# Second MoE's combined weights in rings of their own, loads two steps ahead of the sums, and an eight-column rope scratch

## The chip, the cores and the metric

The kernel runs on one core of one Trainium2 chip. The metric is the device time of one launch in microseconds (us), the median of several runs. The engines are named as in the profile: PE (matrix), PEld (its weight loads), DVE (vector), ACT (scalar), POOL (GpSimd) and SP, which issues nearly all transfers (DMAs). Each engine takes its instructions strictly in the order of its own queue: one that waits holds back everything behind it on that engine.

## The reference

Attention with rotary embedding (4 batches, 8 heads, 576 positions, head size 64), then two feed-forward blocks (MoE here) over 2304 tokens of width 512.

```python
q_rot, k_rot = (rotate(q), rotate(k))                      # rope
attn = softmax(q_rot @ k_rot.T / sqrt(64));  x = attn @ v  # 4 x 8 heads
x = reshape(x, (2304, 512))
h = maximum(maximum(x @ w1, x @ w2), x @ w3)               # first MoE, 768 wide
y = h @ w_out
h = y @ w_in2;  g = h / (1 + exp(-h))                      # second MoE, 2048 wide
out = g @ w_out2
```

Weights arrive as 64-bit floats.

## The kernel before

**Matmuls in halves.** All large products run in fp16 with a high and a low part for each operand, three passes for each product. The second MoE uses seven block products in place of eight (a scheme of Strassen's kind), so its weights are needed as eight 128-column blocks for each piece: four as stored and four sums or differences of these (`SUMS`).

**Attention phase.** `attention()` is a generator over 80 tiles of 128 queries. In each step PE computes the scores of a tile (L424, L427), DVE takes the row maximum (`nb`, L437), ACT the exponentials (`e`, L444), one step later ACT scales them (L456), and from batch 1 on four DMAs and a DVE transpose (`pt`, L495 and L517) turn them for the product with v (`xp`, L558, L562). Between these PE runs groups of the first MoE (`moe1`, L657), whose results are taken out of PSUM by ACT and DVE (`t`, L674 and L676; `h`, L682 and L683; `y`, L700). The PSUM ring of these groups has two banks, so a group waits until the one before the last is taken out.

**Weights prepared beside it.** In the same steps the second MoE's weights are narrowed from 64 bits: `narrow_w2` loads a piece (`z64`), ACT takes its upper half (L228), POOL (L230) and DVE (L239, L240) add lower bits, ACT measures it (`junk`, L154), and it goes to a DRAM scratch, `zwi` for the first weight matrix, `zwo` for the second. When the scale of the first is known, from tile 53 of 80 on, `prep_w8(1.7)` makes the combined weights: 16 items, a new one every 1.7 steps. An item loads four blocks from `zwi` (two DMAs, L950), POOL makes four sums (L926), ACT casts four blocks to the high part (`cast_high`, L930, placed behind the latest exponential), DVE makes the low part (`cast_low`, L934), a DMA stores both in `w8scr` (L961), and the same is done with the four sums. Before the change the eight blocks of an item are one tile `z8` in a ring of two, the first cast goes to `w8o`, which has one buffer, and the second cast goes over the first half of the same `z8` (rows of the profile call `z8` and `z64` both `z`). The offsets of an item's steps are 0 (load), 1 (sums), 1.1 and 2 (first high and low), 2.1 and 3 (second high and low).

**After attention** the last batch's first MoE and then the second MoE (`moe2`, L1053, L1085, L1148) run with PE nearly without a gap; eight loads from `w8scr` (`w8_load`) are issued at the end of attention, and later ones in step with their use.

**Order.** The program is written in the order of these generators; a scheduler then sets each engine's queue, so a transfer or a sum whose inputs are there can stand far ahead of its place in the text. `tc.issue_after(x)` keeps an instruction behind x. A `Ring` hands out its buffers in turn, and a write to a buffer waits for all readers of what was in it.

**Rope.** `qk_rope` loads nothing itself; it rotates q and k of a pair of heads in three parts of 8, 8 and 2 columns of 64 (`rope_steps`: three instructions a part, L353, L354, L357), for batch 0 partly on DVE, else on POOL. Its scratch `w` is one tile of 18 columns.

Of the kernel before, what the change touches and what calls it, by code (L numbers as in the profile page):

```python
# [17 lines left out]
P = 128  # L18
# [4 lines left out]
def fused_kernel(  # L23
# [48 lines left out]
    small = Ring(ctx, "small", 4)  # L72
    junk_p = Ring(ctx, "junk", 1)
# [19 lines left out]
    z8_p, w8o_p = right("z8_p", 2), right("w8o", 1)  # L93
# [88 lines left out]
    class Weights:  # L182
# [68 lines left out]
        def row_max(self, lo=0, n=None, ma=None):  # L251
            ma = ma or self.maxima(lo, n or self.m)
            m1 = small.tile([P, 1], F32, tag="wm1", name="wm1")
            nc.vector.tensor_reduce(out=m1, in_=ma, op=ALU.max, axis=AX.X)
            return m1
# [66 lines left out]
    def v_scale(b):  # L322
        ma = vmax_t.pop(b)
        m = small.tile([P, 1], F32, tag="vm1", name="vm1")
        nc.vector.tensor_reduce(out=m, in_=ma, op=ALU.max, axis=AX.X)
        vmax_t[b] = all_max_a(m)
# [5 lines left out]
    def qk_rope(b, hp):  # L332
        t = raw_t[b, hp]
        w = w_p.tile([P, 18, D], F32, tag="w", name="w")
        if b:
            with tc.issue_after(last["pool"]):
                return rope_steps(t, w, nc.gpsimd, ((0, 8), (8, 16), (16, 18)))
        if hp == 1:
            with tc.issue_after(last["kd"]):
                rope_steps(t, w, nc.vector, ((8, 16), (16, 18)))  # L340
            return rope_steps(t, w, nc.gpsimd, ((0, 4), (4, 8)))
        if hp == 0:
            return rope_steps(t, w, nc.vector, ((8, 16), (0, 8), (16, 18)))
        return rope_steps(t, w, nc.gpsimd, ((0, 8), (8, 16), (16, 18)))

    def rope_steps(t, w, eng, parts):

        tt, at_ = eng.tensor_tensor, lambda c: 4 if c == 16 else c // 2 % 4
        for lo, hi in parts:
            r, v = t[:, lo:hi, :], w[:, lo:hi, :]  # L350
            t4, w4 = (x.rearrange("p (a h) d -> p a h d", h=2) for x in (r, v))
            sin2, cos2 = (x[:, at_(lo):at_(lo) + (hi - lo) // 2, :].unsqueeze(2).to_broadcast([P, (hi - lo) // 2, 2, D]) for x in (sin_sb, cos_sb))
            tt(out=w4, in0=t4, in1=sin2, op=ALU.mult)  # L353
            tt(out=t4, in0=t4, in1=cos2, op=ALU.mult)  # L354
            u4 = r.rearrange("p a (t e) -> p a t e", t=2)
            w4 = v.rearrange("p a (t e) -> p a t e", t=2)
            x = tt(out=u4, in0=u4, in1=w4[:, :, ::-1, :], op=ALU.add)  # L357
        return x
# [577 lines left out]
    def prep_w8(step):  # L936
# [4 lines left out]
        def item(k):  # L941
# [3 lines left out]
            def load():  # L945
                z[0] = z8_p.tile([P, 8, P], F32, tag="z8", name="z8")
                for i in range(2):
                    o = (f + i * HB) * DM
                    x = zscr["wi"][:, o:o + DM].rearrange("p (a c n) -> p a c n", a=2, c=2)[:, :, c]
                    nc.sync.dma_start(out=z[0][:, i:i + 3:2], in_=x)  # L950

            def high(a):
                if a == 0:
                    w[a] = w8o_p.tile([P, 2, 4, P], F16, tag="w8o", name="w8o")
                else:
                    w[a] = flat(z[0][:, 0:4]).bitcast(F16).rearrange("p (x a n) -> p x a n", x=2, n=P)
                cast_high(flat(w[a][:, 0]), flat(z[0][:, a:a + 4]), sw, exps[-1])

            def low(a):
                cast_low(flat(w[a][:, 1]), flat(w[a][:, 0]), flat(z[0][:, a:a + 4]), sw, last["max"])  # L960
# [3 lines left out]
            for d, fn in ((0, load), (1, lambda: combine(z[0], SUMS)), (1.1, lambda: high(0)), (2, lambda: low(0)), (2.1, lambda: high(4)), (3, lambda: low(4))):  # L964
# [279 lines left out]
    wraw = ExitStack()  # L1244
    wraw_p = Ring(wraw, "wraw", 2)

    def pre_down():

        if x_p.get(1) is None:
# [4 lines left out]
            mpools.append(Ring(left, "y_p", 2))  # L1254

# [85 lines left out]
    b_now[0] = 0  # L1341
    attn_pools.close()
# [84 lines left out]
```

## Time and profile before

| | |
|---|---|
| median of 3 runs | 991.97 us (989.47 to 992.7) |
| profiled execution, its own time | 989.2 us |
| its span, first to last instruction | 987.4 us |
| mean granted TensorE clock | 0.974 of full speed |
| busy in the span: PE / DVE / ACT / POOL | 907.6 / 700.4 / 604.0 / 492.2 us |
| attention phase with combined weights being made | about 380 to 569 us |
| first matmul of the second MoE | 644.2 us |

The profile is of one execution; its own time stands 1.8 us above its span, and 2.8 us below the median of the runs. Busy shares are means over stages with different limits, so the argument below goes by stretches and by single waits.

### The profile page before, as it was taken

What the parts mean: (1) busy time and instruction counts of PE and PEld (TensorE: products, weight loads), DVE (VectorE), ACT (ScalarE), POOL (GpSimd) and SP (SyncE); (2) the same over time, 40 slices, a digit from 0 to 9 for tenths busy, and PEclk for the clock granted to TensorE, in tenths of its full rate; (3) what the DMA queues carried; (4) which work ended last, traced back from release to release, by engine and by line L of the source; (5) the groups of instructions that cost most, each with busy time, mean ns of one, the idle gap of its engine ahead of it and who ended that gap; (6) DMA issues with size and microseconds to landing.
All of it is one profiled execution on the core that took longest, in us unless ns stands there. A gap on an engine that the chain in (4) does not pass through costs nothing. (4 is left out here: it accounts for less than half of the span.)

```text
span 987.4 us, 19157 instructions
## 1 busy us (share of the span) xinstructions
PE 907.6 (92%) x6802; PEld 669.8 (68%) x6802; DVE 700.4 (71%) x1231; ACT 604.0 (61%) x1381; POOL 492.2 (50%) x546
## 2 busy tenths in 40 slices
PE   4776998899997999889979899999998999999997
PEld 2343664566664666556645577788887888888886
DVE  5779888777787677868677548764777857856554
ACT  2888577757776677768867625464564544544442
POOL 5835494972546403423233207463678368365264
PEclk9598999999999999999999899999999999999999
DMA  6943035859999775979989673174444344334101
GB/s 155 293 126 106 22 102 132 180 118 198 185 198 188 192 119 134 226 207 216 227 197 198 177 218 113 60 230 133 151 158 133 97 155 134 97 112 135 60 1 43
DMA packets 185198, 146.29 MB, mean 148 GB/s; under 512 B 51216, under 2 KB 168720, under 8 KB 185104
## 3 DMA queue, kind: packets, MB, share of 16 engines
q1 hardware_dynamic: 183600, 144.36, 57.5%
q8 instruction: 54, 0.88, 0.4%
q10 hardware_dynamic: 1504, 0.72, 0.3%
q14 instruction: 40, 0.33, 0.1%
HBM read 90.51 MB, written 26.21 MB: 118 GB/s over the span
## 5 line engine op out<-in xcount | busy, mean ns | idle before, releaser
L657 PEld LDWEIGHTS <-w 128*128 128x128 f16 x1632 | 161.1, 99 | 70.8 <-issue 26.8
L657 PE MATMUL m<-x,w 128*128 128x256 f16 (+1 forms) x1356 | 190.8, 291 | 18.5 <-ACT t L674 10.0
L1148 PEld LDWEIGHTS <-g 128*128 128x128 f16 x1485 | 145.3, 98 | 16.8
L1085 PEld LDWEIGHTS <-w8s 128*128 128x128 f16 x1344 | 131.1, 98 | 16.1 <-issue 0.9
L444 ACT ACTIVATE e<-s,nb 128x576 f32<-128x576 f32 x144 | 105.1, 735 | 34.4 <-DVE nb L437 31.7
L437 DVE TENSOR_REDUCE nb<-s 128x2 f32<-128x1152 f32 (+1 forms) x80 | 98.5, 1232 | 35.2 <-PE s L427 27.1
L926 POOL TENSOR_TENSOR z<-z 128x128 f32<-128x128 f32 (+1 forms) x96 | 62.4, 668 | 121.9 <-DMA z<-zwi 71.9
L456 ACT ACTIVATE e<-e,rec 128x576 f32<-128x576 f32 x144 | 104.1, 767 | 13.9 <-DVE rec L454 13.5
L230 POOL TENSOR_SCALAR z<-z 128x256 uint16<-128x256 uint16 x64 | 51.9, 810 | 107.8 <-ACT z L228 80.6
L562 PE MATMUL xp<-pt,vd 128*64 128x256 f32 (+1 forms) x512 | 79.4, 416 | 0.9 <-DVE pt L517 0.9
L427 PE MATMUL s<-T 64*128 64x512 f32 x256 | 78.6, 684 | 0.0
L517 DVE STREAM_TRANSPOSE pt<-pt 128x1024 f32<-128x1024 f32 (+1 forms) x60 | 67.7, 1128 | 9.7 <-DMA pt<-e 9.7
L1099 POOL TENSOR_TENSOR z<-t 128x256 f32<-128x256 f32 x32 | 27.1, 846 | 87.3 <-DVE t L1091 52.2
L353 POOL TENSOR_TENSOR w<-qk,sin_sb 128x512 f32<-128x512 f32 (+2 forms) x44 | 44.8, 1036 | 41.8 <-DMA qk<-in_q_dram 13.4
L1037 DVE SCALAR_TENSOR_TENSOR g<-gsum,sg,g 128x1024 f16<-128x1024 f32 x36 | 49.1, 1371 | 22.0 <-ACT g L1036 21.6
L657 PE MATMUL m<-h,wo 128*128 128x256 f16 (+1 forms) x448 | 63.9, 292 | 0.4 <-DVE wo L177 0.2
L1036 ACT ACTIVATE g<-gsum,sg 128x1024 f16<-128x1024 f32 x36 | 40.8, 1140 | 36.5 <-POOL gsum L1032 36.5
L657 PEld LDWEIGHTS <-wo 128*128 128x128 f16 x512 | 50.5, 100 | 17.6 <-issue 1.9
L562 PEld LDWEIGHTS xp<-pt,vd 128*64 128x64 f32 x512 | 35.5, 137 | 36.8 <-issue 14.7
L240 DVE SCALAR_TENSOR_TENSOR z<-z,z 128x256 int32<-128x256 int32 x64 | 36.8, 575 | 19.2 <-POOL z L230 18.2
L1148 PE MATMUL b<-w,g 128*128 128x256 f16 x376 | 48.5, 273 | 0.0
L1148 PE MATMUL a<-w,g 128*128 128x256 f16 x376 | 47.9, 273 | 0.0
(254 smaller groups left out, 1956.5 us busy)
## 6 DMA issues: line engine op xcount, KB each, us to landing
w8s<-w8scr SPq DMA_DIRECT2D x64, 448.0 KB, 4.4
pt<-e SPq DMA_DIRECT2D x192, 128.0 KB, 3.9
z<-in_moe_w_in_dram SPq DMA_DIRECT2D x32, 256.0 KB, 3.8
z<-in_moe_w_out_dram SPq DMA_DIRECT2D x32, 256.0 KB, 3.9
w<-in_moe_w_dram SPq DMA_DIRECT2D x6, 768.0 KB, 5.5
wo<-in_moe_w_dram SPq DMA_DIRECT2D x6, 768.0 KB, 4.8
qk<-in_q_dram SPq DMA_DIRECT2D x32, 128.0 KB, 3.4
vd<-in_v_dram SPq DMA_DIRECT2D x16, 256.0 KB, 3.2
```

Source lines behind the costliest of these rows:

```text
L230: nc.gpsimd.tensor_scalar(out=q[:, :, 2], in0=q[:, :, 1], scalar1=step, scalar2=off, op0=ALU.mult, op1=ALU.add)
L427: last["s"] = last["score"] = nc.tensor.matmul(s[:, o:o + 512], qs[r], kt[r], start=True, stop=True).ins
L437: x = nc.vector.tensor_reduce(out=nb[:, 0:m], in_=both(s, 0, 960, 576) if m > 1 else s[:, 0:576], op=ALU.max, axis=AX.X, negate=True)
L444: x = nc.scalar.activation(out=e[:, HK[g]], in_=s[:, SK[g]], func=AF.Exp, bias=nb[:, g:g + 1], accum_out=sm[:, g:g + 1])
L456: nc.scalar.activation(out=e[:, HK[g]], in_=e[:, HK[g]], func=AF.Copy, scale=r[:, g:g + 1])
L517: nc.vector.transpose(out=x, in_=x)
L562: nc.tensor.matmul(xp[r, 0:n], v4[:, g, c, :], turned(c, g), start=False, stop=(c == 3))
L657: x = nc.tensor.matmul(ps[:, 0:n], l, r, start=(first and i == 0), stop=(not more and i == len(passes) - 1))
L926: nc.gpsimd.tensor_tensor(out=z[:, o], in0=z[:, x], in1=z[:, y], op=op)
L1037: nc.vector.scalar_tensor_tensor(out=l, in0=x, scalar=sg_t[jb], in1=h, op0=ALU.mult, op1=ALU.subtract)
L1085: nc.tensor.matmul(o, l, r, start=(i == 0), stop=(i == len(passes) - 1))
L1148: x = nc.tensor.matmul(ps, l, r, start=first, stop=last_, skip_group_check=True)
```

## The change

Four edits, the first three in one function's data:

1. The loaded blocks get a ring of their own, `za` (two buffers of four blocks), the sums another, `zs` (two of four blocks). Nothing is cast over a loaded block any more.
2. Both casts of an item go to `w8o`, which becomes a ring of three, in memory on the other side that is free from `pre_down` on (`w8_out`, closed when attention ends).
3. The steps of an item become 0 (load), 2 (sums), 2.1 and 2.9 (first high and low), 3 and 3.9 (second high and low): the sums stand two steps behind the load instead of one, the last store 0.9 of a step later.
4. Rope's scratch becomes one tile of 8 columns; its three parts take it in turn, for batch 0 together with a `za` and a `zs` buffer. Two one-column tiles move to a ring of one buffer (`rare`).

No instruction is added or removed on any engine: the built programs have 11630, 1233, 1163, 551 and 765 rows for PE, DVE, ACT, POOL and SP in both, counted one by one without register and wait instructions.

```diff
-    z8_p, w8o_p = right("z8_p", 2), right("w8o", 1)
+    za_p, zs_p = right("za_p", 2), right("zs_p", 2)
...
     def qk_rope(b, hp):
         t = raw_t[b, hp]
-        w = w_p.tile([P, 18, D], F32, tag="w", name="w")
+        w = [w_p.tile([P, 8, D], F32, tag="w", name="w")]
+        wide_ = lambda p, nm: p.tile([P, 4, P], F32, tag=nm, name=nm).rearrange("p a n -> p (a n)").rearrange("p (a d) -> p a d", d=D)
+        if b == 0:
+            w = [w[0][:, 0:4], w[0][:, 4:8]] if hp == 1 else w
+            w += [wide_(za_p, "za"), wide_(zs_p, "zs")]
...
-                rope_steps(t, w, nc.vector, ((8, 16), (16, 18)))
+                rope_steps(t, w[2:], nc.vector, ((8, 16), (16, 18)))
...
-        for lo, hi in parts:
-            r, v = t[:, lo:hi, :], w[:, lo:hi, :]
+        for i, (lo, hi) in enumerate(parts):
+            r, v = t[:, lo:hi, :], w[i % len(w)][:, 0:hi - lo, :]
...
             def load():
-                z[0] = z8_p.tile([P, 8, P], F32, tag="z8", name="z8")
+                z[0] = za_p.tile([P, 4, P], F32, tag="za", name="za")
...
+            def sums():
+                z[4] = zs_p.tile([P, 4, P], F32, tag="zs", name="zs")
+                block = lambda i: z[i // 4 * 4][:, i % 4]
+                for o, x, y, op in SUMS:
+                    nc.gpsimd.tensor_tensor(out=block(o), in0=block(x), in1=block(y), op=op)
 
             def high(a):
-                if a == 0:
-                    w[a] = w8o_p.tile([P, 2, 4, P], F16, tag="w8o", name="w8o")
-                else:
-                    w[a] = flat(z[0][:, 0:4]).bitcast(F16).rearrange("p (x a n) -> p x a n", x=2, n=P)
-                cast_high(flat(w[a][:, 0]), flat(z[0][:, a:a + 4]), sw, exps[-1])
+                w[a] = w8o_p[0].tile([P, 2, 4, P], F16, tag="w8o", name="w8o")
+                cast_high(flat(w[a][:, 0]), flat(z[a]), sw, exps[-1])
...
             t = k * step
-            for d, fn in ((0, load), (1, lambda: combine(z[0], SUMS)), (1.1, lambda: high(0)), (2, lambda: low(0)), (2.1, lambda: high(4)), (3, lambda: low(4))):
+            for d, fn in ((0, load), (2, sums), (2.1, lambda: high(0)), (2.9, lambda: low(0)), (3, lambda: high(4)), (3.9, lambda: low(4))):
                 steps.append((t + d, fn))
...
             x_p[1] = Ring(left, "x1", 1)
             mpools.append(Ring(left, "y_p", 2))
+            w8o_p.append(Ring(w8_out, "w8o", 3))
...
     b_now[0] = 0
+    w8_out.close()
     attn_pools.close()
```

The scheduler deals the queues anew. On PE the order is the same up to the transposes of a pair of heads at row 922 of 11630 and again from row 4980 on, which is ahead of the second MoE. Three places follow; the numbers behind a tile's name are its buffer and a running number.

ACT, near the end of attention, around the first cast of item 14 (`w8o` written from a loaded block). Of before:

```order
L930 ACTIVATE z8_1_6106<-z8_1_6106,wihalf_0_4173 128x512
L565 ACTIVATE x_0_5350<-xp_0_6274,vs_3_4988 128x320
L453 ACTIVATE rec_0_6343<-sm_0_6271 128x1
L154 ACTIVATE junk_0_6429,wo2m_0_296<-z_0_6201 128x256
L456 ACTIVATE e_1_6270<-e_1_6270,rec_0_6343 128x576
L930 ACTIVATE w8o_0_6315<-z8_0_6214,wihalf_0_4173 128x512
L507 ACTIVATE pt_0_6176<-tr_1_6351 128x128
L700 ACTIVATE y_0_6541<-m_1_6522,cy_2_5670 128x320
L444 ACTIVATE e_2_6338,sm_1_6339<-s_0_6332,nb_1_6336 128x576 x2
```

The same place of the change:

```order
L449 ACTIVATE e_2_6372,sm_1_6373<-s_0_6366,nb_1_6370 128x576 x2
L512 ACTIVATE pt_0_6212<-tr_1_6385 128x128
L229 ACTIVATE z_2_6393<-z64_2_6240 128x256
L935 ACTIVATE w8o_0_6396<-zs_1_6340,wihalf_0_4187 128x512
L935 ACTIVATE w8o_1_6406<-za_0_6246,wihalf_0_4187 128x512
L458 ACTIVATE rec_1_6454<-sm_1_6373 128x2
L705 ACTIVATE y_0_6583<-m_1_6564,cy_2_5694 128x320
```

The cast of item 14's loaded block (`w8o_0_6315`, now `w8o_1_6406`) stood ahead of the two exponentials of a tile and now stands behind them, next to the cast of item 13's sums, and it takes another buffer than that.

POOL, the sums of item 11 and the narrowings (L230) around them. Of before:

```order
L230 TENSOR_SCALAR z64_1_5624<-z64_1_5624 128x256
L926 TENSOR_TENSOR z8_1_5806<-z8_1_5806 128x128 x4
L230 TENSOR_SCALAR z64_2_5739<-z64_2_5739 128x256
L230 TENSOR_SCALAR z64_3_5800<-z64_3_5800 128x256
L230 TENSOR_SCALAR z64_0_5897<-z64_0_5897 128x256
```

And of the change:

```order
L231 TENSOR_SCALAR z64_2_5763<-z64_2_5763 128x256
L961 TENSOR_TENSOR zs_1_6000<-za_1_5832 128x128 x2
L231 TENSOR_SCALAR z64_3_5826<-z64_3_5826 128x256
L961 TENSOR_TENSOR zs_1_6000<-zs_1_6000,za_1_5832 128x128
L961 TENSOR_TENSOR zs_1_6000<-za_1_5832,zs_1_6000 128x128
```

Two narrowings (`z64_2_5739` and `z64_3_5800`, now `z64_2_5763` and `z64_3_5826`) stood behind all four sums; the first now stands ahead of them and the second between them.

SP, the transfers that feed these rows. Of before:

```order
L950 DMA z8_0_5634<-zwi_0_134 128x2x128 x2
L495 DMA pt_0_5723<-e_2_5599 32x8x128 x4
L961 DMA w8scr_0_133<-w8o_0_5630 128x2x512
L840 DMA z64_3_5800<-in_moe2_w_out_dram 128x256
L821 DMA zwo_0_135<-z_3_5621 128x256
L495 DMA pt_0_5723<-e_0_5701 32x8x128 x4
L961 DMA w8scr_0_133<-z8_1_5572 128x2x512
L840 DMA z64_0_5897<-in_moe2_w_out_dram 128x256
L821 DMA zwo_0_135<-z_0_5736 128x256
L961 DMA w8scr_0_133<-w8o_0_5802 128x2x512
L950 DMA z8_1_5806<-zwi_0_134 128x2x128 x2
```

And of the change:

```order
L845 DMA z64_3_5826<-in_moe2_w_out_dram 128x256
L826 DMA zwo_0_138<-z_3_5649 128x256
L500 DMA pt_0_5747<-e_0_5725 32x8x128 x4
L969 DMA w8scr_0_136<-w8o_0_5770 128x2x512
L955 DMA za_1_5832<-zwi_0_137 128x2x128 x2
```

The load of item 11 (`z8_1_5806`, now `za_1_5832`) stood behind two stores, one of them (`z8_1_5572`) out of the very buffer that the load fills, and seven rows behind the load of `z64_3_5800`. Now it stands four rows behind that load (`z64_3_5826`) and fills a buffer that no store reads.

## Rows read from the trace of the kernel before

**Rows 1.** Page, busy time of each engine in the span.

```profile
PE 907.6 (92%) x6802; PEld 669.8 (68%) x6802; DVE 700.4 (71%) x1231; ACT 604.0 (61%) x1381; POOL 492.2 (50%) x546
```

**Rows 2.** Stretches: PE, PEld, DVE, ACT, POOL busy, PE clock, DMA share, GB/s.

```profile
0.00:100.00 100.00, 65.21 (x306) 36.72 (x308) 74.45 (x128) 70.22 (x153) 57.91 (x61) 0.85 0.61 168
100.00:375.00 275.00, 258.70 (x1740) 167.39 (x1739) 211.40 (x381) 191.76 (x527) 148.57 (x155) 0.99 0.70 148
375.00:575.00 200.00, 180.90 (x1164) 114.52 (x1163) 142.46 (x272) 145.36 (x399) 62.62 (x97) 0.97 0.84 199
575.00:987.40 412.40, 402.75 (x3598) 351.15 (x3595) 272.10 (x454) 196.63 (x303) 223.15 (x233) 1.00 0.38 119
...
450.00:475.00 25.00, 24.95 (x183) 17.05 (x181) 21.13 (x40) 20.99 (x59) 6.90 (x12) 1.00 0.96 222
```

**Rows 3.** Waits, all engines, 375 to 600 us: in total, times, longest.

```profile
POOL z L926 <- DMA z<-zwi: 59.1, 19, 9.0
...
ACT w8o L930 <- DMA w8scr<-w8o: 14.5, 5, 5.5
```

**Rows 4.** Waits of SP's queue, 375 to 600 us.

```profile
SPq L950 <- DMA w8scr<-z: 17.6, 11, 3.5
```

**Rows 5.** The tile `w8o`: casts (ns min/median/max, first and last start), stores to landing.

```profile
L930 ACT ACTIVATE w8o<-z,wihalf x16: 707/721/722, 379.8 to 561.8; 128x512 f16<-128x512 f32 x16
...
DMA to landing us min/median/max: 2.2/3.8/5.0
```

**Rows 6.** Timeline, 400 to 450 us: start, us, engine, [idle before <- releaser].

```profile
416.23 0.72 ACT L930 ACTIVATE w8o<-z,wihalf 128x512 f16<-128x512 f32 x1 [1.92 <-DMA w8scr<-w8o]
...
417.27 2.67 PE L657 MATMUL m<-x,w 128*128 128x256 f16 x12 [1.83 <-ACT t L674]
...
440.19 0.72 ACT L930 ACTIVATE w8o<-z,wihalf 128x512 f16<-128x512 f32 x1 [3.58 <-DMA z<-zwi]
...
441.32 1.47 PE L657 MATMUL m<-x,w 128*128 128x256 f16 x12 [1.01 <-ACT t L674]
...
443.61 0.63 PE L374 MATMUL tr<-ident,qk 128*128 128x128 f32 x4 [0.81 <-ACT pt L507]
```

**Rows 7.** Timeline, 497 to 521 us.

```profile
503.38 3.42 PE L657 MATMUL m<-x,w 128*128 128x320 f16 x24
...
509.24 1.86 POOL L926 TENSOR_TENSOR z<-z 128x128 f32<-128x128 f32 x4 [9.01 <-DMA z<-zwi]
...
511.98 0.43 DVE L240 SCALAR_TENSOR_TENSOR z<-z,z 128x256 int32<-128x256 int32 x1 [3.17 <-POOL z L230]
...
516.94 3.16 PE L657 MATMUL m<-x,w 128*128 128x320 f16 x12 [3.87 <-DVE t L676]
```

**Rows 8.** Timeline, 541 to 556 us.

```profile
541.45 2.06 PE L657 MATMUL m<-h,wo 128*128 128x320 f16 x14
...
550.84 0.72 ACT L930 ACTIVATE w8o<-z,wihalf 128x512 f16<-128x512 f32 x1 [5.50 <-DMA w8scr<-w8o]
...
552.19 0.69 PE L657 MATMUL m<-h,wo1f 128*128 128x320 f16 x2 [4.42 <-ACT y L700]
...
552.67 3.67 PE L657 MATMUL m<-h,wo 128*128 128x320 f16 x13
```

**Rows 9.** Waits of PE, 375 to 600 us.

```profile
PE s L424 <- ACT e L444: 3.9, 4, 1.1
```

**Rows 10.** Timeline, 0 to 45 us: POOL's rope of the third pair of heads.

```profile
17.86 2.90 POOL L353 TENSOR_TENSOR w<-qk,sin_sb 128x512 f32<-128x512 f32 x3 [1.89 <-issue]
```

**Rows 11.** Timeline, 564 to 605 us: last store of combined weights, first loads.

```profile
568.92 0.40 SPq L961 DMA_DIRECT2D w8scr<-z  x1
...
579.58 3.97 SPq L1357 DMA_DIRECT2D w8s<-w8scr  x8
```

**Rows 12.** Timeline, 296 to 330 us.

```profile
316.50 2.67 POOL L926 TENSOR_TENSOR z<-z 128x128 f32<-128x128 f32 x6 [4.93 <-DMA z<-zwi]
...
321.58 3.19 PE L657 MATMUL m<-x,w 128*128 128x320 f16 x12 [4.82 <-ACT t L674]
```

More of the change, by code (lines that the diff above doesn't have):

```diff
@@ L72, in fused_kernel @@
     small = Ring(ctx, "small", 4)
+    rare = Ring(ctx, "rare", 1)
     junk_p = Ring(ctx, "junk", 1)
@@ L252, in row_max @@
             ma = ma or self.maxima(lo, n or self.m)
-            m1 = small.tile([P, 1], F32, tag="wm1", name="wm1")
+            m1 = rare.tile([P, 1], F32, tag="wm1", name="wm1")
             nc.vector.tensor_reduce(out=m1, in_=ma, op=ALU.max, axis=AX.X)
@@ L323, in v_scale @@
         ma = vmax_t.pop(b)
-        m = small.tile([P, 1], F32, tag="vm1", name="vm1")
+        m = rare.tile([P, 1], F32, tag="vm1", name="vm1")
         nc.vector.tensor_reduce(out=m, in_=ma, op=ALU.max, axis=AX.X)
@@ L949, in load @@
                     x = zscr["wi"][:, o:o + DM].rearrange("p (a c n) -> p a c n", a=2, c=2)[:, :, c]
-                    nc.sync.dma_start(out=z[0][:, i:i + 3:2], in_=x)
-            def high(a):
-                if a == 0:
-                    w[a] = w8o_p.tile([P, 2, 4, P], F16, tag="w8o", name="w8o")
-                else:
-                    w[a] = flat(z[0][:, 0:4]).bitcast(F16).rearrange("p (x a n) -> p x a n", x=2, n=P)
-                cast_high(flat(w[a][:, 0]), flat(z[0][:, a:a + 4]), sw, exps[-1])
+                    nc.sync.dma_start(out=z[0][:, i:4:2], in_=x)
+            def sums():
[3 more added lines that the diff above has]
+                    nc.gpsimd.tensor_tensor(out=block(o), in0=block(x), in1=block(y), op=op)
+            def high(a):
+                w[a] = w8o_p[0].tile([P, 2, 4, P], F16, tag="w8o", name="w8o")
+                cast_high(flat(w[a][:, 0]), flat(z[a]), sw, exps[-1])
             def low(a):
-                cast_low(flat(w[a][:, 1]), flat(w[a][:, 0]), flat(z[0][:, a:a + 4]), sw, last["max"])
+                cast_low(flat(w[a][:, 1]), flat(w[a][:, 0]), flat(z[a]), sw, last["max"])
                 nc.sync.dma_start(out=w8scr[:, f, c, :, a:a + 4], in_=w[a])
             t = k * step
-            for d, fn in ((0, load), (1, lambda: combine(z[0], SUMS)), (1.1, lambda: high(0)), (2, lambda: low(0)), (2.1, lambda: high(4)), (3, lambda: low(4))):
+            for d, fn in ((0, load), (2, sums), (2.1, lambda: high(0)), (2.9, lambda: low(0)), (3, lambda: high(4)), (3.9, lambda: low(4))):
                 steps.append((t + d, fn))
@@ L1243, in fused_kernel @@
     mpools = [Ring(left, "h1_p", 8), Ring(left, "tmp_p", 4)]
-    wraw = ExitStack()
+    wraw, w8_out, w8o_p = ExitStack(), ExitStack(), []
     wraw_p = Ring(wraw, "wraw", 2)
```

## The prediction

> **What bounds the kernel now.** The page first: PE is busy 907.6 of 987.4 us [rows 1], so the rest of the span, 79.8 us, is all that any reordering can win, unless it also raises PE's clock. Next the stretches [rows 2], to see where those 79.8 us lie: 34.8 in the first 100 us, 16.3 up to 375, 19.1 between 375 and 575, 9.7 behind it. From 575 us on PE is 98% busy at full clock; nothing that the change touches runs there. The combined weights are made in the third stretch, so that is the one to read. One part of it shows what the other engines can carry: from 450 to 475 us PE is busy 24.95 of 25.00 us while DVE and ACT are at 21.13 and 20.99. So DVE and ACT, at 71% and 73% over the stretch, are no bound; PE stops there for single late results.
>
> Then the waits [rows 3, 4], to see what the combined weights do to the queues. Three things stand out between 375 and 600 us. ACT waits 14.5 us in five pieces for a store out of the one `w8o` buffer. POOL's sums wait 59.1 us for their loads. SP's loads wait 17.6 us for the second store of an item, since that store reads the buffer that the load fills. None of these counts by itself: ACT and POOL have idle time. What counts is whether PE stops behind them, and that is read in the timeline, backward from each stop of PE.
>
> - **A, 417 us** [rows 6]. ACT stands 1.92 us at a cast until the store before it has landed; the evacuation of a matmul group (`t`) stands behind it; PE waits 1.83 us for that. The 12 matmuls that follow take 2.67 us, where the same 12 take 1.47 at 441 us: 1.20 us of lower clock.
> - **B, 440 us** [rows 6]. ACT stands 3.58 us at a cast for its load; PE waits 1.01 us for `t` and 0.81 us for `pt`, both queued behind. No lower clock follows.
> - **C, 517 us** [rows 7]. POOL stands 9.01 us at the four sums of item 11, then needs 1.86 us for them, while two narrowings whose data are there stand behind. DVE waits 3.17 us for the first of these and PE then 3.87 us for DVE's `t`. The 12 matmuls behind take 3.16 us, half of the 24 at 503 us 1.71: 1.45 us of clock.
> - **D, 552 us** [rows 8]. ACT stands 5.50 us at a cast for a store; `y` stands two instructions behind; PE waits 4.42 us. The 15 matmuls behind take 0.69 + 3.67 us, where 14 such take 2.06, 15 thus 2.21: 2.15 us of clock.
>
> **The change part by part.**
>
> *w8o in three buffers, no cast over the loaded blocks.* An item writes two `w8o` tiles in 1.7 steps, so a buffer comes round after 2.55 steps; its store is issued 0.8 or 0.9 of a step after the cast. A step in this stretch is about 7.1 us: the first casts of the 16 items start from 379.8 to 561.8 us [rows 5], 15 x 1.7 = 25.5 steps apart. That leaves some 1.7 steps, 12 us, for a store that lands 2.2 to 5.0 us after issue [rows 5]. So ACT's 14.5 us go. That takes away A and D: 1.83 + 4.42 us of stop and 1.20 + 2.15 of clock, 9.60 us. The Trainium skill (DMA: Bandwidth & Descriptors, "Anatomy of one DMA") puts a transfer of this kind at 2.0 us fixed, mostly the receipt of the last write, plus bytes over 436 GB/s, fitted on GpSimd's path; 256 KB would land in an estimated 2.6 us, and by it the five stops would be some 6 us shorter together. The measured median is 3.8 us, so the page is too low here, and the sum goes by the rows.
>
> *Sums two steps behind the load, load into a buffer that no store reads.* The load of item k+2 now waits for the first low part of item k (offset 2.9 against 3.4), not for its second store. That ends SP's 17.6 us, or turns them into shorter waits for DVE. ACT's first cast of an item stands 2.1 steps behind its load instead of 1.1, some 14 us against a wait that was 3.58 at worst: B goes, 1.82 us. On POOL the order shows a smaller step: the scheduler still puts the sums as far ahead as it can. But the narrowings that stood behind item 11's sums now stand ahead of or between them, and the load stands four transfers behind the narrowing's own, not seven. So POOL's 59.1 us shrink and don't vanish. For C I take what DVE itself waited for POOL, 3.17 of PE's 3.87 us, and the clock, 1.45: 4.62 us. All four stops: 9.60 + 1.82 + 4.62 = 16.0 us.
>
> *Casts and low parts in the same step.* The distance from cast to low part shrinks from 0.9 to 0.8 of a step. DVE's part needs ACT's, and both stand behind the tile's exponentials, so where both fall into one step DVE may wait for ACT. I cost this at nothing, since 0.8 of a step is 5.7 us. Uncovered it is a cast, 0.72 us [rows 6], for each pair.
>
> *The end.* An item's last store comes 0.9 of a step later. The last stands at 568.92 us now, so near 575.3; the first loads of combined weights are issued at 579.58 [rows 11], and the second MoE starts at 644.2. Nothing, with 4 us of cover at the loads and 60 behind them; without cover, the 6.4 us that it is later.
>
> *Rope.* The same instructions with a smaller scratch. In the first stage POOL's third pair stands 1.89 us idle, while DVE reads the scratch that it needs [rows 10]; with buffers of their own these go. PE next waits there for ACT, not for POOL, so I take nothing, and up to 1.89 us as the bound. Later parts use one scratch in turn on one engine; that costs no wait on another.
>
> **How much of 16.0 us comes back.** Upper bound: all, as the 450 us stretch lets PE run full at higher loads of DVE and ACT than the mean. Lower bound: none, if the next late result stops PE at once. Near the stops others wait already: four stops for an exponential, 3.9 us in all [rows 9], stay, and behind a vanished stop of ACT the exponentials still need DVE's maximum. I take 10 of 16.0, nearer the upper end because the row nearest to a run without stops is the 450 us one. Profiled execution: 989.2 - 10 = 979 us; its own time stood 2.8 us below the median, so the forecast for a median is **982 us**.
>
> **The rivals.**
>
> *Hidden anyway.* The casts' stalls only fill time in which ACT would have waited for DVE. For it: in A and B ACT's wait is longer than PE's by 0.1 to 1.8 us, so part is hidden already. Against it: D, 5.50 of ACT against 4.42 of PE. It gives 0 to 3 us: 990.
>
> *More than the four stops.* The `pt` transfers stand behind SP's 17.6 us, and the exponentials behind ACT's casts; if the 3.9 us [rows 9] and rope's 1.89 also go: 992 - 16.0 - 3.9 - 1.9 = 970.
>
> *Slower: a sum ahead of a narrowing in a worse place.* This chain exists outside the four stops and the change leaves it: at 316.5 us POOL waits 4.93 us for the load of items 0 and 1, which the scheduler put far ahead; and PE 4.82 for `t`, whose evacuation stands behind a narrowing's last part, and 12 slow matmuls take 3.19 instead of 1.71 [rows 12], 6.3 us in all. POOL, ACT and PE are dealt anew for 4058 of PE's 11630 rows, and sums still stand between narrowings. For it: 19 waits for loads in the third stretch, the longest 9.0 us [rows 3]. Against it: loads come earlier now. It decides from the point where three such chains stand where none stood: 3 x 6.3 = 18.9 against 10 gives 992 + 9 = 1001; two give 994.6 and leave it even.
>
> *The change doesn't do it.* `w8o` could wait for memory that another pool held, or sums for the new loads; ACT's waits for stores would then stand near 14.5 us again: 992. I count it with the first.
>
> **How the numbers follow.** About half of the stops comes back or more, but not beyond them (975 to 988): 0.50, the forecast. More than that, 970: 0.15. Hidden or not done, 990: 0.22. Slower, 995 to 1001: 0.13. A difference of 0.3% (3 us) is about what a measurement of this kernel can tell from no change; so faster is 0.50 + 0.15 and the few of the third case that win over 3 us, 0.03: 0.68; same 0.19; slower 0.13. The likeliest one's own range is 975 to 988; with cases of the other kinds until 2 in 10 are out, 970 to 995.
>
> **What would show it.** Right: no wait of ACT's `w8o` for a store, SP's wait for `w8scr` stores gone, POOL's wait for `zwi` under 40 us, PE's idle time between 375 us and the end of attention under 10 us, and the stop at 321 us still there. Wrong: ACT waits for stores at other casts, or PE's stops keep their sum with other releasers (`e` for `t`). The forecast fails most likely in the share that comes back.

## The result and the profile after

The changed kernel takes 977.63 us (median of 4 runs, 973.25 to 979.76), the kernel before 991.74 in the same comparison: a ratio of 0.986, 95% interval 0.983 to 0.989, or 14.1 us less. The profiled execution has a span of 975.0 us against 987.4.

Busy times on the page after, against [rows 1]: PE's fell by 3.7 us, which is clock, since the instructions are the same in number.

```profile
PE 903.9 (93%) x6802; PEld 669.8 (69%) x6802; DVE 701.0 (72%) x1231; ACT 604.8 (62%) x1381; POOL 491.9 (50%) x546
```

The stretches after, in the columns of [rows 2] (the last one ends with the span):

```profile
0.00:100.00 100.00, 65.81 (x303) 37.19 (x304) 77.08 (x125) 69.25 (x150) 58.82 (x61) 0.90 0.60 168
100.00:375.00 275.00, 260.08 (x1737) 168.69 (x1738) 206.01 (x381) 191.87 (x529) 149.27 (x155) 0.97 0.70 148
375.00:575.00 200.00, 189.41 (x1321) 125.68 (x1319) 153.29 (x292) 150.03 (x409) 64.45 (x99) 1.00 0.90 220
575.00:975.00 400.00, 388.58 (x3446) 338.23 (x3445) 264.63 (x434) 193.60 (x296) 219.38 (x232) 0.99 0.36 112
```

In the third stretch PE is idle 10.6 us, not 19.1, and its clock is 1.00, not 0.97. But these stretches are cut at fixed times, and the kernels are at other work there. Better cuts are two places that stand at the same point of the work in both: the 12 matmuls behind the stop at 321 us [rows 12], and the first matmul of the second MoE. The same stretches of PE alone (busy, clock, DMA share, GB/s), before:

```profile
0.00:321.58 321.58, 270.49 (x1681) 0.95 0.66 154
321.58:644.03 322.45, 302.11 (x2064) 0.97 0.73 174
644.03:987.40 343.37, 334.96 (x3059) 1.00 0.37 118
```

and after:

```profile
0.00:321.85 321.85, 272.74 (x1682) 0.95 0.66 154
321.85:629.87 308.02, 294.53 (x2064) 0.99 0.76 183
629.87:975.00 345.13, 336.62 (x3059) 0.99 0.38 117
```

The number of matmuls in each stretch is the same but for one, so they can be compared: +0.3, -14.4 and +1.8 us. In the middle one PE's idle time fell from 20.3 to 13.5 us and its busy time, for the same 2064 matmuls, by 7.6: in this pair of traces about half of the gain is stops, the other half clock. In a second pair of traces (below) the idle time of this stretch fell by the same 6.9 us and the busy time by 5.3.

Waits between 375 and 600 us, which answer to [rows 3]:

```profile
POOL zs L961 <- DMA za<-zwi: 19.3, 9, 6.4
```

No wait of ACT's casts for a store is left (one exponential waits 0.8 us that the trace puts down to such a store), and the waits of SP's loads for the second stores [rows 4] have no row any more. The stores land as before (`w8o`, to be held against [rows 5]), the last being issued from 551.2 us:

```profile
L969 SPq DMA_DIRECT2D w8scr<-w8o x32: 359/507/572, 390.6 to 551.2; - x32
...
DMA to landing us min/median/max: 2.2/3.6/5.3
```

Two stops show what is left. The first answers to [rows 12] and has not changed: POOL's sums wait for the load, PE for `t`.

```profile
316.91 0.46 POOL L961 TENSOR_TENSOR zs<-za 128x128 f32<-128x128 f32 x1 [4.65 <-DMA za<-zwi]
...
321.85 3.36 PE L662 MATMUL m<-x,w 128*128 128x320 f16 x12 [5.14 <-ACT t L679]
```

The second is new, in the rest of the first MoE behind the attention. ACT stands at a cast of combined *output* weights (L935, here of `prep_w7`) until their load has landed, with `h` behind it, and PE waits for `h`; 68.3 us pass from the first `mg` matmul to the second MoE, where it was 64.8.

```profile
588.49 0.94 ACT L935 ACTIVATE w<-z,wohalf 128x768 f16<-128x768 f32 x1 [5.06 <-DMA z<-zwo]
589.33 0.40 ACT L687 ACTIVATE h<-t 128x256 f16<-128x256 f32 x1
...
589.78 0.58 PE L662 MATMUL m<-h,wo 128*128 128x256 f16 x2 [1.96 <-ACT h L687]
```

### The profile page after: what moved, and what is told of

Read it like the earlier page. It is cut to its first block, busy times and chain, and to the rows that moved or that the text cites. A ratio compares the mean times of both kernels' runs of the same rounds, so it can differ in the third digit from the quotient of the medians.

```text
span 975.0 us, 19148 instructions
## 1 busy us (share of the span) xinstructions
PE 903.9 (93%) x6802; PEld 669.8 (69%) x6802; DVE 701.0 (72%) x1231; ACT 604.8 (62%) x1381; POOL 491.9 (50%) x546
## 5 line engine op out<-in xcount | busy, mean ns | idle before, releaser
L662 PE MATMUL m<-x,w 128*128 128x256 f16 (+1 forms) x1356 | 188.8, 288 | 15.8 <-ACT t L679 10.0
L1156 PEld LDWEIGHTS <-g 128*128 128x128 f16 x1485 | 146.1, 98 | 17.6
L442 DVE TENSOR_REDUCE nb<-s 128x2 f32<-128x1152 f32 (+1 forms) x80 | 98.6, 1233 | 31.4 <-PE s L432 28.0
L461 ACT ACTIVATE e<-e,rec 128x576 f32<-128x576 f32 x144 | 103.9, 766 | 11.3 <-DVE rec L459 10.6
L522 DVE STREAM_TRANSPOSE pt<-pt 128x1024 f32<-128x1024 f32 (+1 forms) x60 | 67.7, 1129 | 10.0 <-DMA pt<-e 10.0
L358 POOL TENSOR_TENSOR w<-qk,sin_sb 128x512 f32<-128x512 f32 (+2 forms) x40 | 42.2, 1056 | 42.0 <-DMA qk<-in_q_dram 24.8
L931 POOL TENSOR_TENSOR z<-z 128x256 f32<-128x256 f32 x32 | 29.4, 947 | 40.7 <-DMA z<-zwo 36.5
L1156 PE MATMUL c<-w,g 128*128 128x256 f16 x376 | 48.8, 277 | 0.0
L1156 PE MATMUL b<-w,g 128*128 128x256 f16 x376 | 48.4, 273 | 0.0
```

Of the source, the lines that this page charges most:

```text
L442: x = nc.vector.tensor_reduce(out=nb[:, 0:m], in_=both(s, 0, 960, 576) if m > 1 else s[:, 0:576], op=ALU.max, axis=AX.X, negate=True)
L461: nc.scalar.activation(out=e[:, HK[g]], in_=e[:, HK[g]], func=AF.Copy, scale=r[:, g:g + 1])
L522: nc.vector.transpose(out=x, in_=x)
L662: x = nc.tensor.matmul(ps[:, 0:n], l, r, start=(first and i == 0), stop=(not more and i == len(passes) - 1))
L1156: x = nc.tensor.matmul(ps, l, r, start=first, stop=last_, skip_group_check=True)
```

## The experiments

The theory: PE's stops A to D came from ACT's waits for stores and loads and POOL's wait for loads; buffers of their own take A and D, the second step between load and sums takes B and C. The rivals: one of the parts does it alone (the buffers, the distance, or rope's scratch), or the waits were only in time that ACT had anyway.

The medians are of runs beside runs of the kernel before on the same chip. That took 991.7 us beside after, 992.5 beside rope, ring3, oldoff and behind, and 990.6 beside one, one_norope, behind_w7 and ring3_behind; kernels of different groups are therefore compared by their ratios. The columns behind are of each kernel's profiled execution: from the start to the 12 matmuls at about 320 us, from there to the second MoE, and the second MoE, each cut at the same work as above (1681 or 1682, 2064 or 2065, and 3059 matmuls in all of them).

| kernel | median us | ratio, 95% interval | to the 12 matmuls | to second MoE | second MoE |
|---|---|---|---|---|---|
| before | 991.7 | 1 | 321.6 | 322.5 | 343.4 |
| before, second trace | 987.8 (one run) | | 321.0 | 321.7 | 343.4 |
| after | 977.6 | 0.986, 0.983 to 0.989 | 321.9 | 308.0 | 345.1 |
| after, second trace | 973.0 (one run) | | 318.4 | 309.5 | 343.5 |
| rope | 987.5 | 0.995, 0.993 to 0.997 | 317.4 | 319.6 | 344.8 |
| ring3 | 975.8 | 0.985, 0.982 to 0.987 | 317.8 | 310.4 | 343.9 |
| oldoff | 981.8 | 0.990, 0.988 to 0.991 | 318.5 | 315.1 | 345.1 |
| one | 987.0 | 0.997, 0.995 to 0.999 | 323.6 | 320.8 | 345.1 |
| one_norope | 990.0 | 0.999, 0.997 to 1.001 | 323.9 | 320.9 | 345.5 |
| behind | 973.3 | 0.980, 0.978 to 0.982 | 317.4 | 308.0 | 345.8 |
| behind_w7 | 968.2 | 0.978, 0.976 to 0.981 | 315.7 | 305.1 | 344.0 |
| ring3_behind | 970.4 | 0.980, 0.978 to 0.982 | 316.0 | 306.4 | 343.6 |

**rope: the smaller scratch alone, in the kernel before.**

```diff
-        w = w_p.tile([P, 18, D], F32, tag="w", name="w")
+        w = [w_p.tile([P, 8, D], F32, tag="w", name="w")]
+        if b == 0:
+            z8 = z8_p.tile([P, 8, P], F32, tag="z8", name="z8").rearrange("p a n -> p (a n)").rearrange("p (a d) -> p a d", d=D)
+            w = [w[0][:, 0:4], w[0][:, 4:8]] if hp == 1 else w
+            w += [z8[:, 0:8], z8[:, 8:16]]
...
-                rope_steps(t, w, nc.vector, ((8, 16), (16, 18)))
+                rope_steps(t, w[2:], nc.vector, ((8, 16), (16, 18)))
...
-        for lo, hi in parts:
-            r, v = t[:, lo:hi, :], w[:, lo:hi, :]
+        for i, (lo, hi) in enumerate(parts):
+            r, v = t[:, lo:hi, :], w[i % len(w)][:, 0:hi - lo, :]
```

> The kernel before with rope's scratch of 8 columns alone (the first block's further scratch lies in the two tiles of eight blocks). The prediction took nothing for this edit and 1.89 us as its bound: 989 to 992 us, no difference that can be told from the kernel before. Rival, the clock that the first 100 us show higher after the change (0.90 against 0.85) and the new deal of PE's order make the gain, and the combined weights little: 978 to 983 us.

987.48 us, 4.9 less by the ratio (2.8 to 6.9): more than the bound that the prediction gave this edit. The timeline of the kernel before shows a place that the prediction had not looked at, a stop of PE for a copy (`kd`) that DVE makes after a maximum, a transposition and a narrowing's part:

```profile
189.68 1.34 DVE L437 TENSOR_REDUCE nb<-s 128x2 f32<-128x1152 f32 x1
190.95 1.23 DVE L517 STREAM_TRANSPOSE pt<-pt 128x1024 f32<-128x1024 f32 x1
192.10 0.93 DVE L239 TENSOR_SCALAR z<-z 128x256 int32<-128x256 int32 x1
192.96 0.45 DVE L397 COPY kd<-tr 64x64 f32<-64x64 f32 x2
...
193.55 0.30 PE L506 MATMUL tr<-ident,e 128*128 128x128 f32 x1 [2.51 <-DVE kd L397]
```

In rope the same copy stands ahead of the maximum, and PE does not stop there:

```profile
188.03 0.46 DVE L402 COPY kd<-tr 64x64 f32<-64x64 f32 x2
...
189.82 1.36 DVE L442 TENSOR_REDUCE nb<-s 128x2 f32<-128x1152 f32 x1 [0.72 <-PE s L432]
```

With one scratch in turn, POOL does each part of rope to its end before the next, and the queues of this stage are dealt anew. In PE's timeline of rope the stops A, C and D are still there (1.51, 3.87, 4.73 us), and so are ACT's waits for stores: 6.8 us in four pieces, and 5.40 us at stop D, which the trace puts down to a `pt` transfer (the store there was issued at 540.81 us and took 3.5 to land, just when the cast starts, at 544.37).

```profile
413.04 1.47 PE L662 MATMUL m<-x,w 128*128 128x256 f16 x12 [1.51 <-ACT t L679]
511.54 1.79 PE L662 MATMUL m<-x,w 128*128 128x320 f16 x12 [3.87 <-DVE t L681]
545.73 0.69 PE L662 MATMUL m<-h,wo1f 128*128 128x320 f16 x2 [4.73 <-ACT y L705]
```

But the 12 matmuls behind A and C take 1.47 and 1.79 us here, at full clock, and took 2.67 and 3.16 before. That is 2.6 us of clock that the scratch does not explain; the last two runs take it up.

**ring3: rope's scratch and three buffers of narrowed blocks, old distances, sums in the loaded tile of eight blocks.**

```diff
-                if a == 0:
-                    w[a] = w8o_p.tile([P, 2, 4, P], F16, tag="w8o", name="w8o")
-                else:
-                    w[a] = flat(z[0][:, 0:4]).bitcast(F16).rearrange("p (x a n) -> p x a n", x=2, n=P)
+                w[a] = w8o_p[0].tile([P, 2, 4, P], F16, tag="w8o", name="w8o")
...
+            w8o_p.append(Ring(w8_out, "w8o", 3))
```

> The kernel before with rope's small scratch and with the narrowed blocks in three buffers of their own, so that no cast writes over a loaded block; the sums stay one step behind the load, in the one tile of eight blocks, and casts and low parts keep their old times. If the prediction's terms are right, ACT's waits for a store of combined weights (14.5 us before) and SP's waits for them (17.6) are gone, and with them stops A and D, 9.6 us of the 16.0; at the share of the sum that came back in the whole change, 14.1 of 16.0, that is 8.5 us: about 983 us, 980 to 987. Rival, the two-step distance from load to sums does it and the buffers only fill time that ACT has anyway: 988 to 992, with PE's stops of the same sum at other releasers. Rival, the buffers alone do all of it: 976 to 979.

975.77 us, as fast as the whole change (the intervals 0.982 to 0.987 and 0.983 to 0.989 overlap nearly wholly). The theory's 983 missed; the rival that the buffers do all of it, on top of rope, came out. To see which stops are left, count PE's matmuls of the first MoE (`m`) from the 12 at about 320 us: in the kernel before, A, B, C and D stand behind 384, 468, 768 and 876 of them. In ring3 PE waits for nothing at the first three of these places, though the sums still stand one step behind the load. At C, DVE waits 0.34 us for POOL's narrowing, not 3.17:

```profile
497.92 0.43 DVE L241 SCALAR_TENSOR_TENSOR z<-z,z 128x256 int32<-128x256 int32 x1 [0.34 <-POOL z L231]
```

ACT waits 3.0 us in all for loads of combined weights and nowhere for a store of them. (New stops stand elsewhere: 1.51 us behind 432 matmuls, 1.16 ahead of C.) Yet D is there, behind 876 and as long as ever, with another wait behind it:

```profile
536.76 1.25 DVE L522 STREAM_TRANSPOSE pt<-pt 128x1024 f32<-128x1024 f32 x1 [4.11 <-DMA pt<-e]
...
538.09 1.44 ACT L461 ACTIVATE e<-e,rec 128x576 f32<-128x576 f32 x2 [4.15 <-DVE rec L459]
...
540.10 0.69 PE L662 MATMUL m<-h,wo1f 128*128 128x320 f16 x2 [5.25 <-ACT y L705]
```

These are the timelines of DVE, ACT and PE in ring3: `y` is now behind exponentials that wait for a reciprocal, which stands behind a transposition that waits for its `pt` transfer. In the kernel before, a `pt` transfer was late at this place too, by DVE's timeline:

```profile
550.28 1.25 DVE L517 STREAM_TRANSPOSE pt<-pt 128x1024 f32<-128x1024 f32 x1 [3.40 <-DMA pt<-e]
```

It landed by 550.28, and the store that ACT's cast waited for by 550.84 [rows 8]: two late results 0.6 us apart. But `y` was held by the store alone there: it stood two instructions behind the cast, and the exponentials ahead of the cast had been scaled by 545.4. Only the new order of ACT's queue puts `y` behind the transposition. In the changed kernel a first `y` stands ahead of those exponentials (538.03 against 539.92 us), and PE doesn't stop.

**oldoff: the changed kernel with the old distances.**

```diff
-((0, load), (2, sums), (2.1, lambda: high(0)), (2.9, lambda: low(0)), (3, lambda: high(4)), (3.9, lambda: low(4)))
+((0, load), (1, sums), (1.1, lambda: high(0)), (2, lambda: low(0)), (2.1, lambda: high(4)), (3, lambda: low(4)))
```

> The changed kernel with the steps of an item as they were (sums one step behind the load, casts at 1.1 and 2.1, low parts at 2 and 3), and all its buffers. By the prediction's terms A and D stay away, B and C (1.82 + 4.62 us) can come back: 977.6 + 6.4 x 14.1/16.0 = 983 us, 979 to 986; ACT's waits for the loads or POOL's for them grow from 19.3 us towards 59. Rival, the buffers did all of it: 976 to 979, with POOL's waits as after the change. Rival, the distance did nearly all of it: 988 to 992.

981.81 us, within the range expected, but not for the reason given. None of the four stops comes back: PE waits for nothing behind 384, 468, 768 or 876 matmuls. POOL's waits for loads fell further; what grew is its wait for a free buffer of sums, which the second low part of two items earlier still reads (6.3 us after the change). One cast of ACT waits 2.2 us for a store. Its waits in oldoff between 375 and 560 us:

```profile
POOL zs L961 <- DVE w8o L939: 15.5, 4, 8.8
POOL zs L961 <- DMA za<-zwi: 12.0, 8, 4.0
```

Ring3, with the same distances and one tile for loads and sums, has no such wait and is faster (0.982 to 0.987 against 0.988 to 0.991). So the second step seems to be needed by the two separate buffers of sums, not by the loads. Of the 4.7 us between oldoff and ring3 in the stretch to the second MoE, the part that this wait makes was not measured by itself.

**one: the changed kernel with one buffer of narrowed blocks; one_norope: that with rope's scratch as before** (the edit of rope, undone).

```diff
-            w8o_p.append(Ring(w8_out, "w8o", 3))
+            w8o_p.append(Ring(w8_out, "w8o", 1))
```

> The changed kernel with one buffer of narrowed blocks instead of three. Each item's second cast (3 steps) is then written 0.1 step behind the store of its first tile (2.9), which lands 3.6 us after issue at the median; the steps of an item keep their distances. If the wait for stores is what the buffers removed, it comes back on ACT in more pieces than the five of before (up to 16, one for each item), and with it stops like A and D, 9.6 us or more: 985 to 998 us. Rival, those waits only fill time in which ACT would wait anyway: 976 to 980, with ACT's waits for stores long and PE's stops as after the change.

986.95 us: 9.3 more than with three (0.997 against 0.986), and the theory's waits, in 14 pieces between 375 and 560 us:

```profile
ACT w8o L935 <- DMA w8scr<-w8o: 23.8, 14, 3.4
```

PE's stops come back, behind exponentials (`e`) this time; the timeline of one at two of them:

```profile
430.78 0.72 ACT L935 ACTIVATE w8o<-za,wihalf 128x512 f16<-128x512 f32 x1 [3.36 <-DMA w8scr<-w8o]
...
433.86 0.80 PE L429 MATMUL s<-kd,T 128*128 128x128 f32 x2 [3.01 <-ACT e L449]
...
530.24 0.72 ACT L935 ACTIVATE w8o<-za,wihalf 128x512 f16<-128x512 f32 x1 [2.84 <-DMA w8scr<-w8o]
...
534.66 0.80 PE L429 MATMUL s<-kd,T 128*128 128x128 f32 x2 [4.89 <-ACT e L449]
```

At the second, DVE's low part waits 3.41 us for that cast, the row maximum stands behind it, and the exponentials wait for the maximum. So the waits did not fill time that ACT had anyway, and the buffers, not the distance, remove them. This is harder than the kernel before, where the one buffer took 16 casts and not 32; a run with two buffers was not made.

> The kernel of the run named one, with rope's scratch as it was before (18 columns, one tile for all three parts). Rope's edit alone was worth 5.0 us in the kernel before (2.8 to 6.9). If that is its own, by the order that POOL and DVE are dealt between 180 and 200 us (before, PE stood 2.51 us at 193.55 us for a copy of DVE; with the small scratch no such stop), this kernel is 3 to 7 us slower than one, and the stop near 193 us is there. Rival, the 5.0 us were the lower clock falling on other stretches, or the deal of later stages: within 3 us of one.

989.98 us, 3.0 more than one, the low end of what was expected; the intervals (0.997 to 1.001 and 0.995 to 0.999) overlap, so the time alone decides nothing. The stop stands in PE's timeline:

```profile
195.08 0.30 PE L507 MATMUL tr<-ident,e 128*128 128x128 f32 x1 [2.51 <-DVE kd L398]
```

It is in all three traces with the old scratch (2.51, 2.37, 2.51 us) and in none of those with the new.

**behind: the changed kernel with the sums held behind the newest narrowing; behind_w7: that and the first casts of the output weights later.**

```diff
-                    nc.gpsimd.tensor_scalar(out=q[:, :, 2], in0=q[:, :, 1], scalar1=step, scalar2=off, op0=ALU.mult, op1=ALU.add)
+                    last["zn"] = nc.gpsimd.tensor_scalar(out=q[:, :, 2], in0=q[:, :, 1], scalar1=step, scalar2=off, op0=ALU.mult, op1=ALU.add).ins
...
+                with tc.issue_after(last["zn"]):
                     for o, x, y, op in SUMS:
                         nc.gpsimd.tensor_tensor(out=block(o), in0=block(x), in1=block(y), op=op)
```

> The changed kernel with one edit: the four sums of an item are queued on POOL behind the newest narrowing that was written ahead of them. The stop of PE at 322 us (5.14 us of wait, and 12 matmuls in 3.36 us at the lower clock instead of 1.79) is put down to six sums of items 0 and 1 that stand ahead of two narrowings and wait 4.65 us for their load. If that is its cause, it goes, and 6.7 us with it less what comes back: 971 to 974 us. Rival, the narrowings are late for another reason (their own load or the cast ahead of them), or another late result stops PE at the same place: 976 to 979 us.

973.26 us, as expected (0.978 to 0.982 against 0.983 to 0.989). In its trace PE, DVE, ACT and SP have the same instructions in the same order as in the changed kernel; only POOL's order differs. In its timeline the wait of 5.14 us is down to 1.50, and the 12 matmuls run at full clock:

```profile
317.38 1.79 PE L662 MATMUL m<-x,w 128*128 128x320 f16 x12 [1.50 <-ACT t L679]
```

In behind_w7 the steps of `prep_w7` change too:

```diff
-(1, lambda: high(0, 3)), (2, lambda: low(0, 3))
+(2.5, lambda: high(0, 3)), (3.5, lambda: low(0, 3))
```

> The kernel of the run named behind, with the first cast and low part of each combined output weight 1.5 steps later (2.5 and 3.5 instead of 1 and 2). In the changed kernel ACT stands 5.06 us at such a cast for its load (to 588.49 us), an evacuation (h) stands behind it, PE waits 1.96 us for that and runs at a lower clock after: the stretch from the last attention block to the second MoE took 68.3 us against 64.8 before. With the cast later, h stands ahead of it: that stretch 64.5 to 66.5 us, and the kernel at 969 to 971.5 us. Rival, the next late result (the sums on POOL, or the other cast) stops PE as long: 973 to 975.

968.17 us, a little under what was expected. But its interval (0.976 to 0.981) overlaps that of behind (0.978 to 0.982), so the medians alone don't show the gain; the stretch does. It is given here for PE (busy, clock, DMA share, GB/s), from its first `mg` matmul to the second MoE, in behind_w7:

```profile
556.09:620.72 64.63, 64.07 (x512) 1.00 0.40 131
```

and in behind, with one matmul more in the record:

```profile
556.77:625.33 68.56, 65.81 (x513) 0.98 0.37 123
```

The stop of 1.87 us for `h` is gone, and the rest is clock. This version has the lowest median, 0.978 of the kernel before. The stretch also takes 64.6 us in ring3 and ring3_behind, where that cast is not moved and no matmul waits behind it, so the stop belongs to the changed kernel's queues: after, after_again and behind have it. (oldoff takes 67.7 us without it, 2 us of them at a lower clock.)

**ring3_behind: ring3 with the sums held behind the newest narrowing**, by the edit of behind, in `combine`.

> The kernel of the run named ring3 (own buffers, old distances, sums in the loaded tile) with the sums queued on POOL behind the newest narrowing. Its stop at 317.8 us (4.84 us, and 12 matmuls in 3.36 instead of 1.79) goes: 6.4 us, at the share that the same edit gave in the changed kernel (4.4 of 6.7) 4.2: 971.6 us, 969 to 973.5. Rival, with the sums one step behind the load and pinned behind the narrowings, the casts and the store of an item are late and ACT's casts wait for POOL, so that the two-step distance is needed: 974 to 980.

970.37 us, as expected; its interval overlaps those of behind and behind_w7. With the narrowings ahead of the sums, the old distances and one tile for loads and sums do no harm. Its stop D is still 5.24 us. Nothing in these runs shows the second step to be needed for anything but the split.

**Second traces of both kernels, unchanged.**

> The kernel before, unchanged, for a second trace. Open is whether the lower clock behind stops A, C and D (1.20, 1.45 and 2.15 us in the prediction) belongs to the stops or to the execution: the run named rope kept the stops (1.51, 3.87 and 4.73 us) and showed no lower clock behind A and C. If it belongs to the stop, the 12 matmuls behind A and C take 2.67 and 3.16 us again, within 0.1. Rival, it differs from execution to execution of the same program: one of them takes about 1.47 or 1.79 us, and the same instruction of the first 300 us stands 1 to 4 us earlier or later.

The rival came out in the main. In PE's timeline of the second trace, behind C, after the same wait of 3.87 us, the 12 matmuls took 2.68 us instead of 3.16, and A was hardly there at all (D was, 4.66 us):

```profile
415.76 1.47 PE L657 MATMUL m<-x,w 128*128 128x256 f16 x12 [0.17 <-ACT t L674]
...
514.41 2.68 PE L657 MATMUL m<-x,w 128*128 128x320 f16 x12 [3.87 <-DVE t L676]
```

> The changed kernel, unchanged, for a second trace. The runs named after, one and oldoff have the same instructions on each engine up to the first casts of combined weights, and yet the same two matmuls of scores stand at 300.79, 302.35 and 298.39 us. If that is the clock of the execution, they stand elsewhere again in this trace by more than 0.5 us, with the same waits and another granted clock in the first 100 us (0.90 then). The stop at 321.85 us (5.14) stays, and ACT again waits nowhere for a store of combined weights. Rival, the position belongs to the program: 300.8 within 0.3.

The two matmuls of scores stood at 297.18 us, 3.6 earlier, after the same wait (0.97 instead of 0.96), and the granted clock of the first 100 us was 0.86. The stop at the 12 matmuls was there (5.28 us). ACT's casts waited 0.2 us in all for a store of combined weights, and one exponential 0.8.

## Why the prediction was right, and where not

Forecast 982 us, measured 977.6, 0.986 of the time before. The mechanism held: buffers of their own end the waits for stores, and the stops go. That the sum came so near is in part luck, since B, C and D were not taken away by the parts that it named, and the term for rope was missed. By the prediction's steps:

- **The stores and loads.** Right: no wait of ACT's casts for a store, SP's 17.6 us gone, POOL's 59.1 down to 19.3 (it said under 40). ring3 has the whole gain with the buffers and rope's scratch alone, and `one` loses it with a single buffer. The split of loads and sums and the second step, taken together, brought nothing beyond that which these runs show.
- **The four stops, 16.0 us.** All four are gone after the change; their division among the parts was wrong. A was one of two forms that the same program takes (1.83 and 0.17 us). B and C were put down to the second step, but ring3 and oldoff, without that step, have neither. D was put down to the store, but ring3 has no such wait and stops there for 5.25 us, behind a `pt` transfer. It is gone in the changed kernel and in oldoff, which share the split of loads and sums; after the change the transpositions wait 2.6 us at most for `pt`. Why the split has that effect, beyond the new order of the queues, stays open.
- **How much of it comes back.** The prediction kept 10 of 16.0. Between medians the change gained 14.1, of which rope's edit, taken as nothing, makes 4.9 by itself in the kernel before. If it is worth that beside the other edits too (one against one_norope gives 3.0, with overlapping intervals), some 9 to 11 are left for the stops, near the 10: then rope is the term that was missed, and the share was right. In the traces the middle stretch gained 14.4 us in the first pair and 12.2 in the second. In both, idle time fell 6.9 us. In the first the stops counted 11.24 (1.83 + 1.01 + 0.81 + 3.17 + 4.42), so 4.4 came back; the largest new stops are 2.10 us for an exponential at 507, the 1.96 for `h` at 590 shown above, 1.55 for DVE's `t` at 554, 1.49 for a `y` whose buffer waited for its own store at 485 and 1.10 for a `t` at 428. The clock gave 7.6 us and 5.3 where 4.80 were counted: of D's lower clock only the first 15 matmuls had been priced, and between 555 and 560 us it was still 0.77.
- **Rope.** Wrong: taken as nothing, at most 1.89 us, from the one idle time of POOL that the edit removes (it does: in rope POOL starts that pair at 15.34 us, not 17.86). Its measured worth in the kernel before is 4.9 us (2.8 to 6.9), of which the stop near 193 us is 2.4 to 2.5 (the rest is no more than the clock differs between traces, and stays open); the prediction's words "the same instructions with a smaller scratch" passed over the order in which POOL works them off.
- **Casts and low parts in the same step.** Right at nothing: DVE's low parts show no wait for their casts after the change.
- **The end.** Right at nothing, but it was not used: the last store was issued from 551.2 us, 11.4 before the first load at 562.56, so it did not come later against its reader.
- **The chain at 316 us** stays, as said. Held behind the narrowings it was worth 4.4 us between medians (977.6 and 973.3) and 5.6 by the ratios.
- **The slower rival.** Three places where a late load holds a result would have decided it. One appeared, not with POOL's sums but with ACT's casts of output weights at 588 us: 68.3 us against 64.8, 3.5 us lost, of which the stop is 1.96 and most of the rest lower clock. behind_w7 moves that cast and gets them back (68.6 to 64.6 within that pair).
- PE's idle time between 375 us and the end of attention came to 10.6 us, just over the 10 named.

The profiled pair understated the change (12.4 us against 14.1 between medians): the second MoE took 345.1 us instead of 343.4 for one reason given below, and in the second pair (spans of 986.0 and 971.3) that difference was absent.

## What to carry to other kernels

Before counting a stop as gone, look for other late results near it that a new order of the queue could put ahead of the stopped one: without the store, D came back as long behind a late `pt` transfer. To see which stops a change removed, compare places by the count of matmuls, not by time. An edit that "only shrinks scratch" changes the order in which the parts are worked off; look for stops of the bounding engine near every place where it does, not only at the idle time that it removes. An in-order engine should not be given work ahead of its data: two small pins (sums behind the narrowing, a cast 1.5 steps later) took the changed kernel from 0.986 to 0.978 of the time before.

## What the hardware showed that was not expected

**The lower clock falls in other places in each execution of the same instructions.** The kernels after, after_again, oldoff and one have the same instructions up to the first casts of combined weights, and reach the 12 matmuls at 321.9, 318.4, 318.5 and 323.6 us: 5.2 us apart. Between the last and after_again PE's idle time up to there is the same within 0.4 us (48.4 and 48.8), and its busy time for the same matmuls is 275.2 and 269.6. The clearest case stands in the second MoE, which the change doesn't touch. PE stops there 2.63 to 2.65 us for DVE in every trace. After:

```profile
748.79 0.27 PE L122 MATMUL m<-ident,ym 128*1 128x128 f32 x1 [2.63 <-DVE t L1099]
748.90 0.60 PE L1156 MATMUL a<-w,g 128*128 128x256 f16 x4
749.33 2.65 PE L1156 MATMUL c<-w,g 128*128 128x256 f16 x12
751.77 1.35 PE L1156 MATMUL d<-w,g 128*128 128x256 f16 x6
```

and in the second trace of the same kernel:

```profile
746.76 0.27 PE L122 MATMUL m<-ident,ym 128*1 128x128 f32 x1 [2.65 <-DVE t L1099]
746.87 0.60 PE L1156 MATMUL a<-w,g 128*128 128x256 f16 x4
747.30 1.47 PE L1156 MATMUL c<-w,g 128*128 128x256 f16 x12
748.61 0.82 PE L1156 MATMUL d<-w,g 128*128 128x256 f16 x6
```

The granted clock of the `c` and `d` matmuls and the three behind them, in the one and in the other (columns of PE as above):

```profile
749.33:753.00 3.67, 3.67 (x21) 0.54 0.00 0
```

```profile
747.30:749.40 2.10, 2.10 (x21) 1.00 0.00 0
```

18 matmuls take 4.00 us at the lower of the two levels in the one and 2.29 at full clock in the other, 1.7 us for nothing in the program. The same 12 matmuls took 1.47 us in six of the twelve traces and 2.10 to 2.65 in the other six, and the second MoE 343.4 to 344.0 and 344.8 to 345.8 us. So a term for the clock behind one stop is a chance, not a price, and single traces of this kernel differ by several us. The Trainium skill (TensorE: Matmul & The Clock Gate, "What's actually happening") says of the start of a kernel that the gate follows a time base which the kernel does not start, so that the same kernel shows another number of slow matmuls from run to run. The traces agree that the number differs between runs of the same instructions, and they show it behind stops in the middle of a kernel.

**A store of 256 KB landed about as in the prediction's rows.** The median was 3.8 us before, 3.6 after and 3.3 with one buffer (there 2.1 to 6.0). The estimate of 2.6 us by the Trainium skill (DMA: Bandwidth & Descriptors, "Anatomy of one DMA"), from a fit for transfers that GpSimd issues, was below the median of all of these runs, whose stores SP issues; single stores landed in 2.1.
